# Attention, mixer and MLP kernel on one core: block sums written into V by ScalarE for every pair, and the second products moved one step later

## The chip, the core and the metric

The kernel runs on one NeuronCore of a Trainium2 chip. The metric is the device time of one execution in microseconds (us), the median of several runs. The engines have queues of their own and work through them in order: PE (TensorE, matrix products; its weight loads are a row of their own, PEld), ACT (ScalarE), DVE (VectorE), POOL (GpSimd) and SP (SyncE, which here issues nearly all DMAs). An instruction that waits holds up everything behind it on its engine.

## The reference

```python
def _attn_ref(q, k, v):                      # B, H, S, D = 2, 8, 768, 64
    block, window = (32, 16)
    k_sum = k.reshape(B, H, nb, block, D).max(axis=3)
    v_sum = v.reshape(B, H, nb, block, D).mean(axis=3)
    scores_l = scale * np.matmul(q, k.transpose(0, 1, 3, 2))      # kept where |i - j| < window
    scores_s = scale * np.einsum('bhsd,bhnd->bhsn', q, k_sum) + np.log(block)
    a = softmax over the local and the block scores together (+ 1e-09 below the line)
    return np.matmul(a, np.concatenate([v, v_sum], axis=2))

def _moe_ref(x, w_tok1, w_tok2, w_ch1, w_ch2):                   # d_tok, d_ch = 256, 1536
    h = np.maximum(x.transpose(0, 2, 1) @ w_tok1, 0.0) @ w_tok2
    u = x + h.transpose(0, 2, 1)
    return u + np.maximum(u @ w_ch1, 0.0) @ w_ch2

def _moe2_ref(x, g_ln, w_ch1, w_ch2):
    xn = layer norm of x, times g_ln
    return x + np.maximum(xn @ w_ch1, 0.0) @ w_ch2               # 512 -> 2048 -> 512
```

The output is `_moe2_ref(_moe_ref(attention))`. The weights arrive as 64-bit values.

## The kernel before

**Two stages.** First comes attention, woven with the token mixer of the first half; then a long run of products for the two MLPs. The 2 x 8 heads are worked off as 8 pairs (i = 0 to 7), two heads at a time, and each pair in three steps of 256 queries; so there are 24 steps (n = 0 to 23, pair i has n = 3i to 3i+2). What is called scores(n), exp(n) and so on below is the work of step n.

**One step.** PE multiplies Q by K and the block maxima of K into `scores` (16 matmuls, line 297). DVE adds the mask and takes the minimum (`sn`, `mn`, line 317), ACT takes the exponentials (`pr`, four instructions, line 327), PE transposes them (`pt`, line 334), ACT copies them to SBUF (`PT`, line 341, "evac"), PE multiplies them by V (`av`, 16 matmuls, line 354), DVE divides (`u`, line 371), and ACT and POOL split the result in a high and a low part (`xh`, `xl`, lines 385 and 394).

**V and the block sums.** V of a pair lies in one of three buffers, 121 rows x 2 sides x 6 windows. 96 rows of each side are loaded by DMA; the other 24 are the means of V over blocks, the same in all 6 windows. For them POOL adds up the transposed V (`VT`, line 252) into `Z`, PE transposes `Z` into PSUM (`psv`, line 261), and then: for pairs 0 and 1, ACT writes V directly with four instructions, one for each side and head (line 265); for pairs 2 to 7, ACT writes a small tile `VS` (line 274), and two DMAs on SP's queue repeat it over the 6 windows (line 281). Column 64 of those rows holds ones, for the sum of the weights.

**Weights.** They come in 62 halves of 512 KB (`stage`, line 165), through three buffers. Each half needs an ACT instruction (`dec`, line 113), four on DVE (lines 127, 129, 131, 135), one more on ACT (`wh`, line 175) and one more on DVE (`wl`, line 182). Half h+3 can be asked for only when line 135 of half h is done.

**The order** of PE, ACT, DVE and POOL in attention is written out by hand: every piece of a step has an offset in the table `ORDER`, the piece of step n stands at n + offset, and everything is sorted by that number. `evac` 1.4 and `av` 1.95 mean that the copy stands before exp of the next step (n + 1.5) and that av(n) stands before scores(n+2). SP's queue is not written out by hand. With each normalisation up to `ops` conversion pieces of the weights are woven in on DVE and ACT. From `bg` on, products of the token mixer (`g`, lines 198 to 200; the first pieces use the first three halves of weights) fill PE's free time; until then PE gets idle products with a constant tile (`fill`, `warm_ps`, line 616), two and three a step.

Of the kernel before, what the change touches and what calls it, by code (L numbers as in the profile page):

```python
# [10 lines left out]
F32 = mybir.dt.float32  # L11
F32R = mybir.dt.float32r
U32 = mybir.dt.uint32
AF = mybir.ActivationFunctionType
# [4 lines left out]
P = 128  # L19
B, H, S, D = 2, 8, 768, 64  # L20
BLOCK, WINDOW = 32, 16
NB = S // BLOCK
# [4 lines left out]
NK = 96 + NB  # L27
# [4 lines left out]
LEAD = 3  # L32
NXN = 3
ORDER = {
    "load_k": -5.2, "load_vt": -5.1, "load_v": -5.0, "kmax": -1.3, "copy_k": -1.0, "vsum": -2.4,
    "vput": -0.2, "vsum0": 0.6, "vput0": 1.12, "exp": 0.5, "tr": 1.1, "evac": 1.4, "av": 1.95,
    "norm": 2.6, "hi": 2.65, "lo": 2.7, "conv": 3.5, "bg": 9.3, "fin": 0.9,
}
GN = GT * P
NG = B * ST // GT  # L40
# [12 lines left out]
class Kern:  # L53
# [202 lines left out]

    def prep_v2(self, i):
        nc = self.nc
        V, Z, VS = self.V[i % 3], self.Z[i % 2], self.VS[i % 2]
        ps = self.ps_pt.tile([P, 512], F32, tag="pt", name=f"psv{i}")  # L260
        nc.tensor.transpose(ps[:NK, 0:P], Z, self.ident)
        if i < 2:
            for a, j in ((0, 0), (96, 1)):
                for r in range(2):
                    nc.scalar.activation(
                        V[a : a + NB, j, :, 65 * r : 65 * r + 64],
                        ps[a : a + NB, r * 64 : r * 64 + 64]
                        .rearrange("p (o n) -> p o n", o=1)
                        .to_broadcast([NB, 6, 64]),
                        AF.Copy,  # L270
                        scale=1.0 / BLOCK,
                    )
            return
        nc.scalar.activation(
            VS.rearrange("p (r c) -> p r c", r=2)[:, :, 0:64],
            ps[:NK, 0:P].rearrange("p (r c) -> p r c", r=2),
            AF.Copy,
            scale=1.0 / BLOCK,
        )
        for a, j in ((0, 0), (96, 1)):  # L280
            nc.sync.dma_start(
                V[a : a + NB, j, :, 0:129],
                VS[a : a + NB, 0:129].rearrange("p (o n) -> p o n", o=1).to_broadcast([NB, 6, 129]),
            )

    def att_qk(self, n):
# [274 lines left out]
    def attention(self):  # L561


        npair, nq = B * NPAIR, 3 * B * NPAIR
        O = ORDER
        ev = []
        put = lambda at, *fns: ev.append((at, len(ev), fns))
        for i in range(npair):
            at = 3 * i
            if i > 1:  # L570
                put(at + O["load_k"], lambda i=i: self.load_pair(i))
                put(at + O["load_vt"], lambda i=i: self.load_vt(i))
                put(at + O["load_v"], lambda i=i: self.load_v(i))
            put(at + (O["kmax"] if i != 1 else -0.45), lambda i=i: self.prep_k(i))
            put(at + (O["copy_k"] if i != 1 else -0.44), lambda i=i: self.copy_k(i))
            put(at + O["vsum"] if i else O["vsum0"], lambda i=i: self.prep_v1(i))
            put(at + O["vput"] if i else O["vput0"], lambda i=i: self.prep_v2(i))
        for n in range(nq):
            put(n, lambda n=n: self.att_qk(n))
            if n < O["bg"]:  # L580
                put(n + 0.02, lambda: self.fill(2))
                put(n + 0.15, lambda: self.fill(3))
            put(n + O["exp"], lambda n=n: self.att_exp(n))
            put(n + O["tr"], lambda n=n: self.att_tr(n))
            put(n + O["evac"], lambda n=n: self.att_evac(n))
            put(n + O["av"], lambda n=n: self.att_av(n))
            put(n + O["norm"], lambda n=n: self.weave(self.att_norm(n), self.convert(self.ops)))
            put(n + O["hi"], lambda n=n: self.att_hi(n))
            put(n + O["lo"], lambda n=n: self.att_lo(n))
        put(0.0, lambda: self.load_half(0), lambda: self.load_half(1))  # L590
        put(O["conv"], lambda: setattr(self, "ops", 3))
        put(O["bg"], lambda: setattr(self, "ops", 2))
        x0, x1, w0, w1 = self.g1(0, 0), self.g1(0, 1), self.g1(1, 0), self.g1(1, 1)
        y, z0 = self.g2(0), self.transpose_u(0)
        pieces = [x0, x0, x1, x1, y, y, y, y, w0, w0, z0, z0, z0, y, z0, w1, w1, y]
        low = {x0: 5 + O["lo"], x1: 11 + O["lo"], w0: 17 + O["lo"], w1: 23 + O["lo"]}
        need = {x0: 3, x1: 3, w0: 3, y: 6}
        at = O["bg"]
        for k, g in enumerate(pieces):
            while at < low.get(g, 0):  # L600
                at += 1
            if g in need:
                put(at, lambda g=g: self.convert_until(need[g]))
            put(at, lambda g=g: self.begin(g))
            put(at + O["fin"], lambda g=g: self.end(g))
            at += 1
        for _, _, fns in sorted(ev, key=lambda e: e[:2]):
            for fn in fns:
                fn()
        while self.evacs:  # L610
            self.end(self.evacs[0])
# [21 lines left out]
    def run(self):  # L633
        tc, nc, ctx = self.tc, self.nc, self.ctx
# [26 lines left out]
        att = self.att  # L661
# [1 line left out]
        self.K = [att.tile([P, 7, 184], F32, name=f"K{i}") for i in range(3)]  # L663
        self.PT = [att.tile([NK + 1, 512], F32, name=f"PT{i}") for i in range(2)]
        self.V = [att.tile([NK + 1, 2, 6, VC], F32, name=f"V{i}") for i in range(3)]
        self.VS = [att.tile([NK, 130], F32, name=f"VS{i}") for i in range(2)]
        self.VT = [att.tile([P, S], F32, name=f"VT{i}") for i in range(2)]
        self.Z = [att.tile([P, NK], F32, name=f"Z{i}") for i in range(2)]
        self.u = const.tile([P, B * ST, C], F32, name="u")
# [9 lines left out]
        nc.vector.memset(self.warm, 0.0)  # L679
        for t in self.Z:  # L680
            nc.gpsimd.memset(t, 0.0)
        for t in self.V[:2]:
            nc.gpsimd.memset(t[0:NB, 0, :, 64:65], 1.0)
            nc.gpsimd.memset(t[96:NK, 1, :, 64:65], 1.0)
        for t in self.VS:
            nc.gpsimd.memset(t[:, 64:65], 1.0)
        for t in self.PT:
            nc.vector.memset(t[96 : NK + 1], 1.0)
        self.load_pair(0, nc.scalar)
# [45 lines left out]
        for n in range(len(units) + 1):  # L735
# [3 lines left out]
            if n < len(units):  # L739
                kind, s, f, g = units[n]  # L740
                nf = F1 if kind == "u" else F2
                c = 3 + f if kind == "u" else 3 + F1 + f
# [117 lines left out]
```

## Time and profile before

| | |
|---|---|
| time, median of 3 runs | 607.97 us (607.54 to 608.3) |
| profiled execution | 609.79 us, its span 608.0 us |
| PE busy | 581.4 us, 96% of the span |
| DVE busy | 334.8 us, 55% |
| ACT busy | 202.3 us, 33% |
| POOL busy | 42.5 us, 7% |
| mean granted TensorE clock | 0.983 of full speed |

The span is what the profile sees of one execution, from the first instruction to the last; the time of that execution holds 1.8 us more around it. Attention ends about 107 us after the start, and nearly everything behind it is PE at full clock without a gap. So the shares of the whole page are those of the long last part, and attention has to be read by stretches.

### The profile page before, as it was taken

Reading aid. Unit: us, or ns where it says so; the run is one execution under the profiler, and the core shown is the slowest. Engines: PE = TensorE matmul, PEld = TensorE weight load, DVE = VectorE, ACT = ScalarE, POOL = GpSimd, SP = SyncE. Lnnn points to the kernel's source line nnn. Section 1 sums busy time; section 2 is a strip of 40 time slices with the busy share of each in tenths; the row PEclk is TensorE's granted clock in tenths of the full one; section 3 lists DMA queues with packets and bytes.
Section 4 is the critical chain, followed back from the end, with each engine's and each line's share of the span. In section 5 each row is a group of like instructions: output and inputs, shape, how many; then the busy total and the mean of one; then the engine's idle time right before and its main releaser. Section 6 shows DMA issues by size and latency. Waiting matters only on the chain.

```text
span 608.0 us, 9196 instructions
## 1 busy us (share of the span) xinstructions
PE 581.4 (96%) x3595; PEld 507.7 (84%) x3601; DVE 334.8 (55%) x847; ACT 202.3 (33%) x448; POOL 42.5 (7%) x78
## 2 busy tenths in 40 slices
PE   6849899999999999999999999999999999999997
PEld 2527677779899889999888989999888989999896
DVE  3576995899368799788789951111153211111122
ACT  4665877644133444343444411110122111010110
POOL 0443552000000000000000000000000000000000
PEclk9888899999999999999999999999999999999999
DMA  9996770135324333233423200000000100000011
GB/s 263 310 275 194 240 237 26 43 132 172 105 71 138 105 103 112 98 110 133 137 72 103 71 2 1 0 1 0 1 29 24 53 0 1 1 0 1 0 53 52
DMA packets 23377, 52.70 MB, mean 87 GB/s; under 512 B 2147, under 2 KB 10275, under 8 KB 23334
## 3 DMA queue, kind: packets, MB, share of 16 engines
q1 hardware_dynamic: 23184, 51.71, 27.2%
q8 instruction: 28, 0.46, 0.3%
q10 hardware_dynamic: 150, 0.41, 0.2%
q14 instruction: 15, 0.12, 0.1%
HBM read 48.08 MB, written 3.15 MB: 84 GB/s over the span
## 4 chain that ended last, share of the span: by engine, by line
PE 87%; DVE 6%; DMA 4%; ACT 1%; issue 1%; SPq 0%; ACTq 0%
DMA V<-VS 2%; PE g L198 1%; PE av L354 1%; PE g L200 1%; PE g L199 1%; DMA V<-in_v_dram 1%; DVE sn L317 1%; PE scores L297 1%; PE pt L334 1%; DMA mask<-in_mask_dram 1%; PE warm_ps L616 1%; PE tx L515 1%; DVE dec L135 1%; DVE dec L131 1%; PE acc_('x', 0)_0_3743 L199 1%
## 5 line engine op out<-in xcount | busy, mean ns | idle before, releaser
L113 ACT ACTIVATE dec<-stage 128x512 f32<-128x512 f32 x62 | 41.6, 673 | 11.0 <-DMA stage<-in_wts_dram 11.0
L135 DVE SCALAR_TENSOR_TENSOR dec<-stage,dec 128x512 uint32<-128x512 uint32 x62 | 44.0, 709 | 0.9
L131 DVE SCALAR_TENSOR_TENSOR dec<-stage,dec 128x512 uint32<-128x512 uint32 x62 | 43.8, 706 | 0.9
L175 ACT CAST wh<-dec 128x512 fp32r<-128x512 f32 x62 | 38.0, 615 | 17.1 <-DVE dec L135 16.9
L182 DVE TENSOR_TENSOR wl<-dec,wh 128x512 fp32r<-128x512 f32 x62 | 42.9, 695 | 0.0
L354 PEld LDWEIGHTS av<-V,PT 121*64 121x64 f32 x384 | 15.5, 152 | 23.6 <-issue 12.0
L354 PE MATMUL av<-V,PT 121*64 121x65 f32 x384 | 19.2, 243 | 16.2 <-DMA V<-VS 7.5
L317 DVE CUSTOM_DVE_ANT_0 sn<-scores,mask 128x120 f32<-128x120 f32 x96 | 21.2, 275 | 18.0 <-PE scores L297 18.0
L327 ACT ACTIVATE pr<-sn,mn 128x120 f32<-128x120 f32 x96 | 30.0, 386 | 2.7 <-DVE mn L317 2.6
L129 DVE TENSOR_SCALAR dec<-dec 128x512 uint32<-128x512 uint32 x62 | 28.0, 453 | 1.0
L127 DVE TENSOR_SCALAR dec<-dec 128x512 f32<-128x512 f32 x62 | 26.8, 433 | 1.8 <-ACT dec L113 1.8
L394 POOL TENSOR_TENSOR xl<-u,xh 128x256 fp32r<-128x256 f32 x24 | 18.9, 788 | 44.4 <-ACT xh L385 41.9
L616 PE MATMUL warm_ps<-warm 128*128 128x512 bf16 x59 | 19.2, 441 | 2.0 <-DVE warm L679 1.2
L252 POOL TENSOR_TENSOR VT<-VT 128x384 f32<-128x384 f32 (+3 forms) x28 | 19.0, 680 | 22.2 <-DMA VT<-in_vt_dram 20.6
L341 ACT COPY PT<-pt 120x512 f32<-120x512 f32 x24 | 14.0, 584 | 16.0 <-PE pt L334 15.8
L297 PE MATMUL scores<-K,Q 64*64 64x120 f32 x384 | 16.7, 293 | 1.9 <-ACT K L236 1.7
L334 PE MATMUL pt<-ident,pr 128*120 128x128 f32 x96 | 16.9, 300 | 0.0
L334 PEld LDWEIGHTS pt<-ident,pr 128*120 128x120 f32 x96 | 11.8, 148 | 5.1 <-issue 2.2
L198 PE MATMUL g<-xh,wh 128*128 128x256 f32 x48 | 14.2, 296 | 0.6 <-DVE u L431 0.6
L297 PEld LDWEIGHTS scores<-K,Q 64*64 64x64 f32 x384 | 10.8, 142 | 4.6 <-ACT K L236 2.2
L490 DVE TENSOR_SCALAR xn<-u,mv,rs 128x128 f32<-128x128 f32 x48 | 13.9, 340 | 0.0
L199 PE MATMUL g<-xl,wh 128*128 128x256 f32 x48 | 13.4, 279 | 0.0
(3004 smaller groups left out, 1669.7 us busy)
## 6 DMA issues: line engine op xcount, KB each, us to landing
stage<-in_wts_dram SPq DMA_DIRECT2D x62, 512.0 KB, 3.3
V<-in_v_dram SPq DMA_DIRECT2D x16, 306.0 KB, 8.4
K<-in_k_dram SPq DMA_DIRECT2D x8, 480.0 KB, 6.5
VT<-in_vt_dram SPq DMA_DIRECT2D x8, 384.0 KB, 9.1
out_dram<-u SPq DMA_DIRECT2D x12, 256.0 KB, 2.1
Q<-in_q_dram SPq DMA_DIRECT2D x7, 384.0 KB, 8.5
V<-VS SPq DMA_DIRECT2D x12, 72.6 KB
Q<-in_q_dram ACTq DMA_DIRECT2D x1, 384.0 KB, 3.3
```

What stands on the lines that cost most here:

```text
L113: nc.scalar.activation(m, self.raw[n][:, :, 1].bitcast(F32), AF.Abs)
L127: nc.vector.tensor_scalar(m, m, MAG_LO, MAG_HI, op0=ALU.max, op1=ALU.min)
L129: nc.vector.tensor_scalar(mi, mi, 3, 0x3FFFFFF8, op0=ALU.logical_shift_left, op1=ALU.bitwise_and)
L131: nc.vector.scalar_tensor_tensor(mi, t[:, :, 1], 0xC0000000, mi, op0=ALU.bitwise_and, op1=ALU.bitwise_or)
L135: nc.vector.scalar_tensor_tensor(mi, t[:, :, 0], 29, mi, op0=ALU.logical_shift_right, op1=ALU.bitwise_or)
L175: self.nc.scalar.copy(self.slots[c if c < 16 else c - 16][0][:, s], x)
L182: self.nc.vector.tensor_tensor(wl[:, s], x, f32(wh[:, s]), op=ALU.subtract)
L297: nc.tensor.matmul(ps[cols, j, e, :NK], Q[rows, 64 * w : 64 * w + 64], K.rearrange("p v c -> p (v c)")[rows, a : a + NK], start=True, stop ...
L317: nc.vector.tensor_tensor_reduce(sn[:, u], ps[:, u % 2, u // 2, :NK], self.mask[:, mv], scale=-SCALE, scalar=3e38, op0=ALU.add, op1=ALU.mi ...
L327: nc.scalar.activation(pr[:, u], sn[:, u], AF.Exp, bias=mn[:, u : u + 1], scale=-1.0)
L334: nc.tensor.transpose(ps[:NK, u * P : u * P + P], pr[:, u], self.ident)
L354: nc.tensor.matmul(ps[64 * j : 64 * j + 64, e, 65 * r : 65 * r + 65], pt[:, u * P + 64 * (r ^ j) : u * P + 64 * (r ^ j) + 64], V[:, j, 2 * ...
```

## The change

The block sums of every pair are now written by ACT straight into V, with one instruction a side that covers both heads and all 6 windows (24 x 768 values); `VS`, its two DMAs a pair and its memsets go, and the third V buffer gets its column of ones at the start. In the order, `av` moves from 1.95 to 2.15 and `evac` from 1.4 to 1.55: av(n) now stands behind scores(n+2) and the transposes of step n+1, and the copy of step n behind exp(n+1). The first product pieces of the mixer start at 8.58 instead of 9.3 and end 0.97 instead of 0.9 behind their start, the load of V stands at -4.7 instead of -5.0, each early step has four idle products instead of five, and four conversion pieces a step are woven in instead of three until `bg`, then two as before.

```diff
-    "load_k": -5.2, "load_vt": -5.1, "load_v": -5.0, "kmax": -1.3, "copy_k": -1.0, "vsum": -2.4,
-    "vput": -0.2, "vsum0": 0.6, "vput0": 1.12, "exp": 0.5, "tr": 1.1, "evac": 1.4, "av": 1.95,
-    "norm": 2.6, "hi": 2.65, "lo": 2.7, "conv": 3.5, "bg": 9.3, "fin": 0.9,
+    "load_k": -5.2, "load_vt": -5.1, "load_v": -4.7, "kmax": -1.3, "copy_k": -1.0, "vsum": -2.4,
+    "vput": -0.2, "vsum0": 0.6, "vput0": 1.12, "exp": 0.5, "tr": 1.1, "evac": 1.55, "av": 2.15,
+    "norm": 2.6, "hi": 2.65, "lo": 2.7, "conv": 3.5, "bg": 8.58, "fin": 0.97,
...
         nc.tensor.transpose(ps[:NK, 0:P], Z, self.ident)
-        if i < 2:
-            for a, j in ((0, 0), (96, 1)):
-                for r in range(2):
-                    nc.scalar.activation(
-                        V[a : a + NB, j, :, 65 * r : 65 * r + 64],
...
-        nc.scalar.activation(
-            VS.rearrange("p (r c) -> p r c", r=2)[:, :, 0:64],
...
         for a, j in ((0, 0), (96, 1)):
-            nc.sync.dma_start(
-                V[a : a + NB, j, :, 0:129],
-                VS[a : a + NB, 0:129].rearrange("p (o n) -> p o n", o=1).to_broadcast([NB, 6, 129]),
+            nc.scalar.activation(
+                V[a : a + NB, j, :, 0:130].rearrange("p w (r c) -> p w r c", r=2)[:, :, :, 0:64],
+                ps[a : a + NB, 0:P]
+                .rearrange("p (o r c) -> p o r c", o=1, r=2)
+                .to_broadcast([NB, 6, 2, 64]),
+                AF.Copy,
+                scale=1.0 / BLOCK,
             )
...
                 put(n + 0.02, lambda: self.fill(2))
-                put(n + 0.15, lambda: self.fill(3))
+                put(n + 0.25, lambda: self.fill(2))
...
-        put(O["conv"], lambda: setattr(self, "ops", 3))
+        put(O["conv"], lambda: setattr(self, "ops", 4))
...
-        for t in self.V[:2]:
+        for t in self.V:
             nc.gpsimd.memset(t[0:NB, 0, :, 64:65], 1.0)
             nc.gpsimd.memset(t[96:NK, 1, :, 64:65], 1.0)
-        for t in self.VS:
-            nc.gpsimd.memset(t[:, 64:65], 1.0)
```

**ACT around the block sums of pair 2 (steps 4 to 7).** Before, from the first split of weights to the exponentials of step 6 (`pr_505`) and those of step 7 (`pr_567`):

```order
L175 CAST wh_70<-dec_350 128x512
L113 ACTIVATE dec_413<-stage_352 128x512
L385 CAST xh_116<-u 128x2x128
L236 COPY K_100<-ks_417 128x7x24
L341 COPY PT_101<-pt_440 120x512
L327 ACTIVATE pr_451<-sn_449,mn_450 128x120 x4
L385 CAST xh_116<-u 128x2x128
L274 ACTIVATE VS_106<-psv_470 120x2x64
L341 COPY PT_102<-pt_494 120x512
L327 ACTIVATE pr_505<-sn_503,mn_504 128x120 x4
L175 CAST wh_70<-dec_355 128x512
L113 ACTIVATE dec_524<-stage_410 128x512
```

After, the same stretch, up to the exponentials of step 6 (`pr_497`) and the copy behind them:

```order
L175 CAST wh_70<-dec_340 128x512
L113 ACTIVATE dec_402<-stage_342 128x512
L371 CAST xh_114<-u 128x2x128
L236 COPY K_100<-ks_408 128x7x24
L313 ACTIVATE pr_440<-sn_438,mn_439 128x120 x4
L327 COPY PT_101<-pt_422 120x512
L175 CAST wh_70<-dec_345 128x512
L113 ACTIVATE dec_458<-stage_398 128x512
L371 CAST xh_114<-u 128x2x128
L263 ACTIVATE V_105<-psv_465 24x6x2x64 x2
L313 ACTIVATE pr_497<-sn_495,mn_496 128x120 x4
L327 COPY PT_102<-pt_479 120x512
```

Three things moved: each copy to `PT` stands behind the next step's exponentials, the two wide writes of V stand where the one of `VS` stood, and `dec` of the fourth half of weights (`stage_410` before, `stage_398` after; half 3 when counted from 0) now stands ahead of the exponentials of step 6 instead of behind them.

**PE in steps 10 to 12, around the block sums of pair 4 (`psv`).** There are no idle products here. Before, from the products with V of step 9 (`av_797`) on; the names after `pr` are those of steps 10 and 11:

```order
L354 MATMUL av_797<-V_103,PT_102 64x65 x8
L297 MATMUL scores<-K_98,Q_95 64x120 x8
L334 MATMUL pt_815<-ident,pr_773 120x128 x4
L261 MATMUL psv_841<-ident,Z_110 120x128
L354 MATMUL av_846<-V_103,PT_101 64x65 x8
L297 MATMUL scores<-K_99,Q_96 64x120 x8
L334 MATMUL pt_863<-ident,pr_825 120x128 x4
```

After, from the scores of step 11 on:

```order
L283 MATMUL scores<-K_98,Q_95 64x120 x8
L320 MATMUL pt_796<-ident,pr_760 120x128 x4
L340 MATMUL av_801<-V_103,PT_102 64x65 x8
L261 MATMUL psv_829<-ident,Z_108 120x128
L283 MATMUL scores<-K_99,Q_96 64x120 x8
L320 MATMUL pt_841<-ident,pr_812 120x128 x4
L340 MATMUL av_846<-V_103,PT_101 64x65 x8
```

The products with V of step 9 (`av_797`, now `av_801`) moved behind the scores of step 11 and the transposes of step 10, and those of step 10 behind the scores of step 12 and the transposes of step 11. Of the mixer's products, the first piece now stands between av(6) and `psv` of pair 3, ahead of scores(9), and the second ahead of scores(10); before they stood one step later, behind scores(9) and behind scores(10).

**SP's queue at pair 4.** Before:

```order
L165 DMA stage_410<-in_wts_dram 128x1024
L208 DMA K_99<-in_k_dram 128x6x160
L209 DMA Q_96<-in_q_dram 128x768
L165 DMA stage_466<-in_wts_dram 128x1024
L281 DMA V_105<-VS_106 24x6x129 x2
L213 DMA VT_108<-in_vt_dram 128x768
```

After:

```order
L165 DMA stage_398<-in_wts_dram 128x1024
L208 DMA K_99<-in_k_dram 128x6x160
L165 DMA stage_453<-in_wts_dram 128x1024
L209 DMA Q_96<-in_q_dram 128x768
L213 DMA VT_106<-in_vt_dram 128x768
L165 DMA stage_516<-in_wts_dram 128x1024
```

The two DMAs from `VS` are gone, and the loads of weights stand somewhat further ahead among those of K, Q and VT; the load of half 3 keeps its place behind the same DMAs.

## Rows read from the trace of the kernel before

**Rows 1.** Stretches: length, busy PE, PEld, DVE, ACT, POOL, PE clock, DMA share, GB/s.

```profile
30.00:37.00 7.00, 5.24 (x80) 3.70 (x82) 6.93 (x28) 5.54 (x16) 4.40 (x7) 1.00 1.06 290
37.00:45.20 8.20, 0.68 (x4) 0.12 (x2) 5.40 (x16) 3.71 (x10) 2.90 (x6) 0.77 1.06 272
45.20:51.00 5.80, 5.45 (x41) 3.59 (x42) 3.13 (x14) 1.91 (x7) 0.72 (x1) 0.50 0.53 142
51.00:62.00 11.00, 10.96 (x150) 9.27 (x150) 7.26 (x29) 8.23 (x24) 5.38 (x9) 0.97 0.78 229
62.00:81.00 19.00, 16.04 (x223) 13.60 (x223) 19.00 (x71) 14.69 (x40) 10.90 (x17) 0.91 0.80 236
81.00:100.00 19.00, 18.85 (x270) 15.32 (x268) 15.39 (x73) 13.82 (x41) 7.83 (x12) 1.00 0.50 149
100.00:110.00 10.00, 8.13 (x104) 5.99 (x97) 6.04 (x28) 7.04 (x20) 2.50 (x4) 1.00 0.01 2
```

**Rows 2.** Timeline of PE: start, duration, line, instruction, idle time before and its releaser.

```profile
30.41 0.32 PE L261 MATMUL psv<-ident,Z 128*120 128x128 f32 x1 [0.91 <-POOL Z L255]
...
45.21 1.59 PE L354 MATMUL av<-V,PT 121*64 121x65 f32 x16 [7.53 <-DMA V<-VS]
46.73 1.08 PE L297 MATMUL scores<-K,Q 64*64 64x120 f32 x16
...
51.94 0.64 PE L297 MATMUL scores<-K,Q 64*64 64x120 f32 x16
...
55.98 0.28 PE L200 MATMUL g<-xh,wl 128*128 128x256 f32 x1
```

**Rows 3.** Timeline of SP's DMA issues: start, duration, line, transfer.

```profile
26.64 0.33 SPq L220 DMA_DIRECT2D V<-in_v_dram  x1
29.27 0.35 SPq L165 DMA_DIRECT2D stage<-in_wts_dram  x1
...
34.36 2.60 SPq L281 DMA_DIRECT2D V<-VS  x2
```

**Rows 4.** Timeline of POOL in attention.

```profile
26.65 3.22 POOL L252 TENSOR_TENSOR VT<-VT 128x384 f32<-128x384 f32 x4 [4.62 <-DMA VT<-in_vt_dram]
29.95 0.41 POOL L255 TENSOR_TENSOR Z<-VT 128x24 f32<-128x24 f32 x2
```

**Rows 5.** Timeline of ACT around the block sums of pair 2.

```profile
34.64 1.25 ACT L327 ACTIVATE pr<-sn,mn 128x120 f32<-128x120 f32 x4
...
38.47 0.67 ACT L113 ACTIVATE dec<-stage 128x512 f32<-128x512 f32 x1 [2.06 <-DMA stage<-in_wts_dram]
39.04 0.39 ACT L385 CAST xh<-u 128x256 fp32r<-128x256 f32 x1
39.34 0.58 ACT L341 COPY PT<-pt 120x512 f32<-120x512 f32 x1
39.81 1.25 ACT L327 ACTIVATE pr<-sn,mn 128x120 f32<-128x120 f32 x4
40.97 0.60 ACT L175 CAST wh<-dec 128x512 fp32r<-128x512 f32 x1
44.59 0.66 ACT L113 ACTIVATE dec<-stage 128x512 f32<-128x512 f32 x1 [3.02 <-DMA stage<-in_wts_dram]
```

**Rows 6.** Groups of ACT by line and shape, 0 to 110 us: count, busy us, mean ns.

```profile
L265 ACT ACTIVATE V<-psv 24x384 f32<-24x384 f32 x8 | 3.4, 476 | 1.3 <-PE psv L261 1.2
...
L236 ACT COPY K<-ks 128x168 f32<-128x168 f32 x8 | 2.6, 329 | 1.1 <-DVE ks L226 1.0
...
L274 ACT ACTIVATE VS<-psv 120x128 f32<-120x128 f32 x6 | 1.7, 275 | 0.5 <-PE psv L261 0.4
```

**Rows 7.** What DVE waited for from 25.3 to 94 us: total, times, longest.

```profile
DVE sn L317 <- PE scores L297: 7.1, 3, 5.4
DVE hl L414 <- ACT hh L413: 2.0, 2, 1.3
```

**Rows 8.** What PE waited for from 25.3 to 110 us.

```profile
PE av L354 <- ACT PT L341: 5.6, 8, 1.8
```

More of the change, by code (lines that the diff above doesn't have):

```diff
@@ L258, in prep_v2 @@
         nc = self.nc
-        V, Z, VS = self.V[i % 3], self.Z[i % 2], self.VS[i % 2]
+        V, Z = self.V[i % 3], self.Z[i % 2]
         ps = self.ps_pt.tile([P, 512], F32, tag="pt", name=f"psv{i}")
         nc.tensor.transpose(ps[:NK, 0:P], Z, self.ident)
-        if i < 2:
-            for a, j in ((0, 0), (96, 1)):
-                for r in range(2):
-                    nc.scalar.activation(
-                        V[a : a + NB, j, :, 65 * r : 65 * r + 64],
[L267 to L273, printed above, removed]
-        nc.scalar.activation(
-            VS.rearrange("p (r c) -> p r c", r=2)[:, :, 0:64],
[L276 to L279, printed above, removed]
-        for a, j in ((0, 0), (96, 1)):
-            nc.sync.dma_start(
-                V[a : a + NB, j, :, 0:129],
-                VS[a : a + NB, 0:129].rearrange("p (o n) -> p o n", o=1).to_broadcast([NB, 6, 129]),
+        for a, j in ((0, 0), (96, 1)):
+            nc.scalar.activation(
[5 more added lines that the diff above has]
+                scale=1.0 / BLOCK,
             )
@@ L665, in run @@
         self.V = [att.tile([NK + 1, 2, 6, VC], F32, name=f"V{i}") for i in range(3)]
-        self.VS = [att.tile([NK, 130], F32, name=f"VS{i}") for i in range(2)]
         self.VT = [att.tile([P, S], F32, name=f"VT{i}") for i in range(2)]
```

## The prediction

> **What bounds the kernel now.** I read the table of stretches first [rows 1], because the page's shares are those of the long last part: there PE is busy without a gap, none of its instructions changes, and only the moment at which attention lets go of it counts. The reader is to see four kinds of stretch. From 30 to 37 us DVE is full (6.93 of 7.00 us). From 37 to 45.2 PE does almost nothing (0.68 us) while the DMA engines are full. From 62 to 81 DVE is full again (19.00 of 19.00). From 81 to 100 PE is (18.85 of 19.00).
>
> The timeline of PE names the hole [rows 2]: av(6), the first products that use pair 2's V, wait 7.53 us for the two DMAs from `VS`. These were issued from 34.36 on [rows 3] and had landed at 45.21. They move little, but stand in the queue behind bulk loads. After the hole PE's granted clock is 0.50, the lower level of 1.2 GHz, up to 51 us [rows 1]. The third view is who waits for whom on DVE [rows 7]: from 25.3 to 94 us it stood still for scores or for `hh` for 9.1 us in all (7.1 + 2.0), 5.4 of them in this hole. So 9.1 us is all that could be had there while DVE's work stays as it is.
>
> **What the change removes.** Twelve DMAs on SP, and with them the 7.53 us wait. The Trainium skill (DMA: Bandwidth & Descriptors, Anatomy of one DMA) fits one DMA, on the path from GpSimd, as about 2.0 us plus bytes / 436e3; for 72.6 KB that is an estimate of 2.2 us, the sums would be in V before PE asks for them, the first term below would be nothing, and the result some 606.5. The rows do not bear that out: 10.85 us passed between issue and release.
>
> **What it adds.** Two ACT instructions of 24 x 768 a pair. No row shows that shape. Of the nearest rows, both from PSUM, 128 values take 275 ns and 384 take 476 ns [rows 6], so one value more costs 0.785 ns, and 768 take 476 + 384 x 0.785 = 777 ns. Two are 1.5 us with a little overlap. From below it is two of the 384-value rows, 0.95 us; from above four of them, 1.9 us. I take 1.5. For pairs 2 to 7 that is 1.2 us more than `VS`, each time ahead of the exponentials; for pairs 0 and 1 some 0.3 us less.
>
> **What it moves, and where the stall goes.** Four conversion pieces a step instead of three put `dec` of weight half 3 ahead of exp(6), and behind it on ACT stand `xh`, the two V writes of pair 2, exp(6) and copy(5); PE's transposes of step 6 wait for that exp, and all that follows on PE for them. Half 3 was asked for at 29.27 [rows 3], and ACT got it at 38.47 after waiting 2.06 us [rows 5]. Before, that `dec` stood behind exp(6), which ran at 34.64. Asking a little earlier hardly helps: the same loads stand ahead of it, V of pair 3 issued up to 26.64 the last [rows 3]. I keep 38.47.
>
> From there, in starting distances of [rows 5]: `dec` 0.57, `xh` 0.30, V 1.5, exp 1.16, so exp(6) ends at 42.0, where before PE was let go at 45.21. Then copy 0.47, `wh` 0.5, `dec` of half 4 0.57, `xh` 0.30, exp 1.16: exp(7) ends at 45.0. Half 4 landed at 44.59; now it stands directly behind K of pair 4, and at the 272 to 290 GB/s of [rows 1] these 1.0 MB take 3.6 us, so it is there at 42.1. Half 5 stands behind Q and VT, 1.3 MB or 4.7 us more: 46.8, 0.8 us after ACT could take it. So `xh`(5) ends at 47.7, POOL's `xl` at 48.4 by the 0.7 us that I estimate for it, and the first product piece of the mixer, now ahead of scores(9), can run from there. Its 2.1 us are an estimate from 18 products of some 0.12 us, and `psv` and scores(9) take 0.9 more: scores(9) is done at 51.4. Before it was done at 52.5 (51.94 + 0.57), and the first product piece at 56.2 [rows 2]. With the transposes of step 8 and av(7), which before stood ahead of that (1.1 us), the new order is there at 52.5. The gain up to here is 3.7; I take 3.5, since PE comes out of a hole of its own at the lower clock too: behind `psv` at 30.7 it has scores(6), transposes, av(4) and scores(7) to do, some 4 us, and then waits from about 35 to 42. Bounds: nothing, and 9.1 us.
>
> Pairs 0 to 2 bring nothing before that: `psv` of pair 2 waits for POOL, POOL for the load of VT, which landed at 26.65, and `Z` was done at 30.36 [rows 2, 4]. None of it is moved.
>
> **From 62 to 81 us.** ACT is busy 14.69 us. Two pairs add 2.4, and the half of weights that is now handled earlier takes some 1.2 away (0.67 + 0.60, [rows 5]): 15.9. DVE loses five pieces of that half, some 3 us (an estimate at the 0.6 of ACT's instructions of that size): 16. PE has 16.04. So the 19 us cannot fall by more than 3. That ACT's copy no longer stands between the transposes and the next exponentials lets the three engines run side by side more, yet three engines that are 85% full get in each other's way: I take half, 1.5, with bounds 0 and 3.
>
> **From 81 to 100** PE is full: nothing. The V writes of pairs 6 and 7 lie beside PE's products there; ACT has 13.82 + 2.4 of 19. Without that cover they cost 2.4; I count 0.5 against. **From 100 to 110** PE is idle for 1.9 us (10.00 - 8.13), mostly for the copy to `PT` [rows 8], which is now off that path: 0.5, bounds 0 and 1.9.
>
> **Counted at nothing.** The 14 idle products that go: until 45 us PE waits anyway, and those of steps 8 and 9 are in the 3.7 above. The memsets: POOL waits for VT then [rows 4]. V's load at -4.7: it has to follow av, which is later by as much, and SP issues it behind the same kind of loads. K's copy (329 ns, [rows 6]) keeps its place ahead of an exp.
>
> **Sum.** 3.5 + 1.5 - 0.5 + 0.5 = 5.0 us. Against the profiled execution: 609.79 - 5.0 = 604.8, its span 603.0. That execution lay 1.8 us above the median of 607.97, so the forecast for the median is 603.0.
>
> **Rivals.**
> *All of it comes back.* Half 3 does not hold ACT up, or ACT has slack enough, and DVE runs full from 25 us on. Then up to 9.1 us return [rows 7] and 0.5 at the end: 607.97 - 9.6 = 598.4. For it speaks that DVE's total does not grow; against it the 2.06 and 3.02 us that ACT already waited for weights [rows 5]. The Trainium skill (DMA: Bandwidth & Descriptors, Queues, rings and completion order) says that each engine takes descriptors in ring order; by that rule half 3 cannot pass what was issued ahead of it, and the trace agrees with 9.2 us from issue to use. Chance 0.20.
> *Swallowed.* PE restarts sooner, but DVE, full from 62 to 81, and ACT with 2.4 us more give it back: -0.5 to +1.0, 607.5. For it speaks [rows 1], against it that DVE's idle time ahead of 62 is now used for weights. Chance 0.12.
> *ACT is the new bound, slower.* Place: `dec` of halves 3 to 5 ahead of exp(6) to exp(8), with V's writes in the same row. From 45.0 on each exp would wait for its half. It decides if half 3 comes after 42.0 (38.47 + 3.5); if half 5 then comes 6.1 us behind half 4, as 4 did behind 3 (44.59 - 38.47), it is there at 50.7 instead of 46.8, scores(9) is done 3.9 us later, and of the 3.7 us nothing is left (-0.2). From 62 to 81 ACT, now the bound, pays the 2.4 us of V writes in full: 607.97 + 0.2 + 2.4 = 610.6. Against it: the DMA engines lose the narrow `VS` transfers, in whose stretch the rate fell from 290 to 272 [rows 1]. Chance 0.11.
>
> **How the numbers follow.** The forecast has 0.57. A measurement of this kernel can tell 0.2% from no change (1.2 us, 606.8 to 609.2). Faster: 0.57 + 0.20 = 0.77; same 0.12; slower 0.11. The range is 598.5 to 607.0: it leaves out the slower case, about half of the swallowed one and the far end of the first rival, some 0.2 in all. The likeliest case alone lies within 600.5 to 605.5.
>
> **What would show it.** Right: no wait on `VS`; V writes of about 0.78 us; ACT waiting for `stage` ahead of exp(6), which ends near 42; a hole on PE from about 35 to 42; scores(9) near 51, with the first product piece ahead of it; the end of attention about 5 us sooner. Wrong: no such wait on ACT (then the first rival), ACT full from 62 to 81 with PE waiting for `pr` (then the second), or V writes well above 1 us.

## The result, and the profile after

The kernel after takes 615.57 us (median of four, 613.32 to 618.51), the kernel before, measured beside it, 608.13 us: ratio 1.0125 (95% interval 1.0101 to 1.0149). It is slower by 1.25%, some 7.6 us, where 5 us less was forecast.

The profiled execution after took 613.32 us, with a span of 611.5; it is the fastest of its four. The one of before [rows 1] took 609.79 us, and all four measured executions of before lie below that. So the two profiles are only 3.5 us apart, less than half of what lies between the medians. The same stretches as in [rows 1], columns as there:

```profile
30.00:37.00 7.00, 3.25 (x42) 1.60 (x40) 5.40 (x19) 2.36 (x5) 0.59 (x1) 0.91 1.05 301
37.00:45.20 8.20, 6.73 (x66) 4.36 (x67) 6.72 (x18) 7.10 (x18) 5.17 (x9) 0.66 0.76 254
45.20:51.00 5.80, 5.80 (x71) 5.18 (x70) 3.65 (x22) 5.63 (x14) 2.16 (x3) 1.00 0.97 350
51.00:62.00 11.00, 5.96 (x93) 4.34 (x92) 8.12 (x33) 7.55 (x22) 2.66 (x7) 0.74 0.75 221
62.00:81.00 19.00, 15.89 (x204) 12.47 (x202) 16.34 (x64) 14.06 (x36) 11.40 (x17) 0.88 0.67 215
81.00:100.00 19.00, 17.94 (x227) 13.55 (x228) 11.62 (x57) 14.57 (x37) 6.28 (x11) 1.00 0.13 35
100.00:110.00 10.00, 8.63 (x126) 6.51 (x126) 5.47 (x28) 7.46 (x21) 2.18 (x3) 1.00 0.01 2
```

The hole of PE from 37 to 45 is gone (6.73 us busy instead of 0.68). A new one stands from 51 to 62: PE is busy 5.96 of 11.00 us there, before 10.96. From 62 to 81 DVE is no longer full (16.34 of 19.00 us, before 19.00), yet PE does no more there than before (15.89, before 16.04).

Start by start the two profiled executions tell the same. Scores(10) begins at 51.06, before at 56.80: 5.7 us ahead. Scores(12) is 2.6 ahead (60.58 against 63.18), scores(15) 1.8 (73.02 against 74.86), scores(17) 1.1 behind (83.19 against 82.08), and the end of attention 3.15 behind (112.92 against 109.77; taken here and below as the start of the first product on `xh` behind the last `u`, line 198). So the lead lies ahead of step 10, 6.8 us of it go between steps 10 and 17, and 2 more from there to the end. The lead is one over a slow execution: in two more of the kernel before, shown further down, scores(10) begins at 50.94 and 54.42. The place of the loss is seen on ACT (start, duration, line, instruction, idle time before):

```profile
48.59 1.63 ACT L263 ACTIVATE V<-psv 24x768 f32<-24x768 f32 x2
50.24 1.25 ACT L313 ACTIVATE pr<-sn,mn 128x120 f32<-128x120 f32 x4
51.52 0.59 ACT L327 COPY PT<-pt 120x512 f32<-120x512 f32 x1
52.00 0.39 ACT L399 ACTIVATE hh<-g 128x256 fp32r<-128x256 f32 x1
53.62 0.40 ACT L371 CAST xh<-u 128x256 fp32r<-128x256 f32 x1 [1.23 <-DVE u L357]
54.42 1.25 ACT L313 ACTIVATE pr<-sn,mn 128x120 f32<-128x120 f32 x4 [0.40 <-DVE mn L303]
55.57 0.56 ACT L327 COPY PT<-pt 120x512 f32<-120x512 f32 x1
56.04 0.38 ACT L399 ACTIVATE hh<-g 128x256 fp32r<-128x256 f32 x1
...
59.94 1.25 ACT L313 ACTIVATE pr<-sn,mn 128x120 f32<-128x120 f32 x4
```

and on DVE in the same time:

```profile
52.42 0.42 DVE L400 SCALAR_TENSOR_TENSOR hl<-g,hh 128x256 fp32r<-128x256 f32 x1 [3.57 <-ACT hh L399]
52.76 0.17 DVE L354 RECIPROCAL rec<-av 128x4 f32<-128x4 f32 x1
52.85 0.40 DVE L129 TENSOR_SCALAR dec<-dec 128x512 uint32<-128x512 uint32 x1
53.16 0.42 DVE L357 TENSOR_TENSOR u<-av,rec 128x256 f32<-128x256 f32 x1
53.50 0.68 DVE L131 SCALAR_TENSOR_TENSOR dec<-stage,dec 128x512 uint32<-128x512 uint32 x1
54.10 0.28 DVE L303 CUSTOM_DVE_ANT_0 sn<-scores,mask 128x120 f32<-128x120 f32 x1
...
56.45 0.42 DVE L400 SCALAR_TENSOR_TENSOR hl<-g,hh 128x256 fp32r<-128x256 f32 x1 [1.46 <-ACT hh L399]
```

`hh` and `hl` take the high and low part of a mixer piece. With `bg` 8.58 and `fin` 0.97 they stand at 9.55: on ACT behind the exponentials (9.5) and behind the copy of the step, on DVE still ahead of `sn` of the next step. So the two engines take turns. DVE waits for `hh`; then come `hl`, the division and two weight pieces, and only then `sn`; ACT meanwhile waits for `sn`. One turn, from exp to exp, takes 4.18 us (50.24 to 54.42), and the next 5.52 (54.42 to 59.94). The kernel before was no quicker in its first turn here:

```profile
54.07 1.26 ACT L327 ACTIVATE pr<-sn,mn 128x120 f32<-128x120 f32 x4
...
58.55 1.25 ACT L327 ACTIVATE pr<-sn,mn 128x120 f32<-128x120 f32 x4
...
62.55 1.25 ACT L327 ACTIVATE pr<-sn,mn 128x120 f32<-128x120 f32 x4
```

Its two turns took 4.48 and 4.00 us, but PE was full with product pieces of the mixer then (10.96 of 11.00 us). In the kernel after the first of these pieces lies behind already, and PE waits with the others:

```profile
51.06 0.64 PE L283 MATMUL scores<-K,Q 64*64 64x120 f32 x16
...
55.05 0.64 PE L283 MATMUL scores<-K,Q 64*64 64x120 f32 x16 [2.14 <-DVE mn L303]
...
60.58 1.08 PE L283 MATMUL scores<-K,Q 64*64 64x120 f32 x16 [2.85 <-ACT pr L313]
...
82.06 0.51 PE L198 MATMUL g<-hh,wh 128*128 128x512 f32 x1 [1.24 <-ACT hh L399]
```

The last row is the second product of the mixer, which needs `hh` at once and holds up scores(17) behind it on PE's queue.

### The profile page after: what moved, and what is told of

Its sections match the earlier page's. It is cut to its first block, busy times and chain, and to the rows that moved or that the text cites. A ratio compares the mean times of both kernels' runs of the same rounds, so it can differ in the third digit from the quotient of the medians.

```text
span 611.5 us, 9137 instructions
## 1 busy us (share of the span) xinstructions
PE 583.8 (95%) x3587; PEld 505.2 (83%) x3587; DVE 334.0 (55%) x847; ACT 210.5 (34%) x450; POOL 41.3 (7%) x78
## 3 DMA queue, kind: packets, MB, share of 16 engines
HBM read 48.08 MB, written 3.15 MB: 84 GB/s over the span
## 4 chain that ended last, share of the span: by engine, by line
PE 84%; ACT 5%; DMA 4%; DVE 4%; issue 1%; POOL 0%; SPq 0%; ACTq 0%; POOLq 0%
ACT pr L313 2%; DMA stage<-in_wts_dram 2%; PE g L198 1%; DMA VT<-in_vt_dram 1%; PE g L199 1%; PE g L200 1%; PE tx L501 1%; PE av L340 1%; DMA mask<-in_mask_dram 1%; ACT PT L327 1%; PE scores L283 1%; PE pt L320 1%; ACT V L263 1%; PE acc_('x', 0)_0_3717 L199 1%; PE acc_('x', 2)_0_4718 L199 1%
## 5 line engine op out<-in xcount | busy, mean ns | idle before, releaser
L283 PEld LDWEIGHTS scores<-K,Q 64*64 64x64 f32 x384 | 10.8, 142 | 17.4 <-DVE mn L303 5.4
L320 PE MATMUL pt<-ident,pr 128*120 128x128 f32 x96 | 18.5, 312 | 5.8 <-ACT pr L313 4.7
L320 PEld LDWEIGHTS pt<-ident,pr 128*120 128x120 f32 x96 | 11.8, 149 | 12.6 <-ACT pr L313 6.9
L602 PE MATMUL warm_ps<-warm 128*128 128x512 bf16 x51 | 17.1, 451 | 1.2 <-DVE warm L664 1.2
L263 ACT ACTIVATE V<-psv 24x768 f32<-24x768 f32 x16 | 12.9, 808 | 4.0 <-PE psv L261 4.0
```

What stands on the lines that cost most here:

```text
L283: nc.tensor.matmul(ps[cols, j, e, :NK], Q[rows, 64 * w : 64 * w + 64], K.rearrange("p v c -> p (v c)")[rows, a : a + NK], start=True, stop ...
L320: nc.tensor.transpose(ps[:NK, u * P : u * P + P], pr[:, u], self.ident)
```

## The experiments

Each version was measured beside the kernel before; ratios are to that, with a 95% interval. The diffs show the numbers or lines that change; the rest of a longer line is left out. Four theories stood at the start. **M**: the mixer's places, `hh` above all, are the loss. **A**: the V writes on ScalarE are. **O**: the fourth conversion piece is. **S**: weight loads on SP's queue behind waiting VT and V loads are.

### Which part of the change costs

**V writes alone.** After, with everything else back (the diff gathers numbers that stand on several lines):

```diff
-"load_v": -4.7, "evac": 1.55, "av": 2.15, "bg": 8.58, "fin": 0.97   # fill 2+2, ops 4
+"load_v": -5.0, "evac": 1.4, "av": 1.95, "bg": 9.3, "fin": 0.9      # fill 2+3, ops 3
```

> Only the V writes by ScalarE are changed; every place in the order, the fills and the conversion pieces a step are those of before. Theory M (the loss lies in the mixer's places: hh now stands behind V writes, exp and copy, and VectorE's hl waits for it): the 7.5 us wait goes and nothing is given back, 601 to 604 us. Theory A (the V writes on ScalarE ahead of every third exp are the loss, 1.6 us a pair): 609 to 614 us, and ScalarE is what PE waits for from 62 to 81 us.

Measured 607.1 us, 0.9992 (0.9969 to 1.0014): both missed. The V writes and the removed wait together change nothing that can be measured.

**New places alone**, V sums over `VS` as before (the diff above the other way round, in the kernel before):

> All places in the order, the fills and the four conversion pieces are those of after; the V sums still go over VS and twelve DMAs. Theory M: the new places cost some 6 us on top of the old wait for VS, 611 to 616 us. Theory A: without the V writes on ScalarE the new places do no harm, 604 to 608.5 us.

Measured 614.05 us, 1.0113 (1.0088 to 1.0138): as M said. The new order (places, fills and pieces) carries nearly all of the loss without any V write, so A falls.

**After with the mixer's old places.**

```diff
-"bg": 8.58, "fin": 0.97,
+"bg": 9.3, "fin": 0.9,
```

> After with the two numbers of the mixer's pieces as before (9.3 and 0.9 in place of 8.58 and 0.97). Theory M: hh stands ahead of the exp of its step again, hl waits about 1.5 us less twice, and the time falls to 603 to 609 us. Theory S (weight loads stand on SP behind VT and V loads that wait for GpSimd and PE) or theory O (a fourth conversion piece a step fills ScalarE and VectorE too early): 612 to 616 us, as after.

Measured 611.12 us, 1.0059 (1.0040 to 1.0077): between the two, about half of the loss.

**After with three conversion pieces.**

```diff
-put(O["conv"], lambda: setattr(self, "ops", 4))
+put(O["conv"], lambda: setattr(self, "ops", 3))
```

> After with three conversion pieces a step up to the mixer, as before. Theory O: the 4.6 us wait of dec ahead of exp(6) and the crowding behind it go, 605 to 610 us. Theory M or S: less weight work is done early, and the time stays at 613 to 617 us.

Measured 611.92 us, 1.0080 (1.0055 to 1.0106): between again. So neither M in this form nor O explains all of it, and the question is whether the parts add up.

### One number

**After with `hh` ahead of the exponentials.** The pieces' products stay where they are.

```diff
-"bg": 8.58, "fin": 0.97,
+"bg": 8.58, "fin": 0.9,
```

> After with one number changed: a mixer piece's hh and hl at 0.90 instead of 0.97 behind its products, which puts hh ahead of the exp and the copy of that step. Theory M: most of what the old mixer's places gave back (4.5 us) comes with this number alone, 609.5 to 612.5 us. Rival: what counts is where the products of a piece stand on PE, and not hh, 614 to 617 us.

Measured 608.62 us, 1.0007 (0.9989 to 1.0026): the whole loss is gone, more than M expected. ACT in this kernel:

```profile
51.96 0.39 ACT L399 ACTIVATE hh<-g 128x256 fp32r<-128x256 f32 x1
53.04 1.25 ACT L313 ACTIVATE pr<-sn,mn 128x120 f32<-128x120 f32 x4 [0.69 <-DVE mn L303]
54.20 0.56 ACT L327 COPY PT<-pt 120x512 f32<-120x512 f32 x1
54.66 0.40 ACT L371 CAST xh<-u 128x256 fp32r<-128x256 f32 x1
54.97 0.38 ACT L399 ACTIVATE hh<-g 128x256 fp32r<-128x256 f32 x1
56.03 1.25 ACT L313 ACTIVATE pr<-sn,mn 128x120 f32<-128x120 f32 x4 [0.69 <-DVE mn L303]
...
59.68 1.25 ACT L313 ACTIVATE pr<-sn,mn 128x120 f32<-128x120 f32 x4
```

and DVE:

```profile
55.38 0.42 DVE L400 SCALAR_TENSOR_TENSOR hl<-g,hh 128x256 fp32r<-128x256 f32 x1 [0.43 <-ACT hh L399]
55.72 0.27 DVE L303 CUSTOM_DVE_ANT_0 sn<-scores,mask 128x120 f32<-128x120 f32 x1
```

The first turn from exp to exp takes 2.99 us instead of 4.18, the second 3.65 instead of 5.52: 6.64 us for both instead of 9.70. `sn` follows `hl` on DVE at once, and the division and the weight pieces run while ACT is at the exponentials. The number `fin` moves `hh` on ACT and `hl` on DVE together; the two were not moved apart. At the second product PE does not wait for `hh` at all.

**The same without V writes**: the new places with `VS` kept, and `fin` 0.9.

> All new places but hh at 0.90, with VS and its DMAs kept and no V write by ScalarE from pair 2 on. Theory M (the place of hh by itself): the 6.6 us of the new places (614.05) come back, 606 to 609.5 us. Rival (hh is late because V writes stand ahead of it; without them its place costs little, and the loss of 614.05 has another cause): 612 to 615 us.

Measured 608.21 us, 1.0003 (0.9983 to 1.0023), as M said. With `VS` and `hh` at 0.97 ACT shows

```profile
53.73 1.24 ACT L327 ACTIVATE pr<-sn,mn 128x120 f32<-128x120 f32 x4
54.87 0.56 ACT L341 COPY PT<-pt 120x512 f32<-120x512 f32 x1
55.33 0.38 ACT L413 ACTIVATE hh<-g 128x256 fp32r<-128x256 f32 x1
...
57.74 1.25 ACT L327 ACTIVATE pr<-sn,mn 128x120 f32<-128x120 f32 x4 [0.40 <-DVE mn L317]
```

and with `hh` at 0.90

```profile
53.69 1.25 ACT L327 ACTIVATE pr<-sn,mn 128x120 f32<-128x120 f32 x4 [0.69 <-DVE mn L317]
...
56.68 1.25 ACT L327 ACTIVATE pr<-sn,mn 128x120 f32<-128x120 f32 x4 [0.69 <-DVE mn L317]
```

a first turn of 4.01 us against 2.99. So the V writes have no part in the loss.

**`hh` early for the first two pieces only.**

```diff
-put(at + O["fin"], lambda g=g: self.end(g))
+put(at + (0.9 if k < 2 else O["fin"]), lambda g=g: self.end(g))
```

> After with hh at 0.90 for the first two mixer pieces alone, and at 0.97 for the other sixteen. If the loss lies at the first two (the trace of after loses its lead from step 11 on, behind their hh): 608 to 611 us. If it lies at the later ones: 613 to 616 us.

Measured 612.2 us, 1.0071 (1.0044 to 1.0099): between. The first two pieces carry 0.54 of the 1.18%, or 3.3 us, which fits the 3.1 us of the two turns; the later ones carry 0.64. Either share is uncertain by some 0.3. The later part shows on PE in this kernel, between scores(16) and scores(17):

```profile
80.32 0.50 PE L198 MATMUL g<-hh,wh 128*128 128x512 f32 x1 [2.61 <-ACT hh L399]
```

### Do the other parts add up?

**After with the old depth.**

```diff
-"load_v": -4.7, "evac": 1.55, "av": 2.15,
+"load_v": -5.0, "evac": 1.4, "av": 1.95,
```

> After with the copy, av and the V load at their old places (1.4, 1.95, -5.0). Theory D: 608 to 612 us. Theory M+O: the mixer's places and the fourth piece are still there, and PE's wait for PT comes back, 615 to 619 us.

Measured 623.04 us, 1.0232 (1.0200 to 1.0263), above what either expected. Theory D (the depth costs) falls; without it PE waits 15.8 us for `PT`, in after 1.4:

```profile
PE av L340 <- ACT PT L327: 15.8, 12, 4.8
```

**V writes and depth, mixer, fills and pieces as before.**

> V writes by ScalarE and the deeper places (copy 1.55, av 2.15, V load -4.7); mixer, fills and conversion pieces as before. Theory M+O (mixer's places and the fourth piece are the whole loss): PE no longer waits 10.8 us for PT as with the V writes alone, and 601 to 606 us come out. Theory D (the depth itself costs, because av, and with it V's release and the next V load, come later): 609 to 613 us.

Measured 608.25 us, 1.0002 (0.9983 to 1.0021): neither. The depth, worth 1.1% in the kernel after, is worth nothing with the mixer, fills and pieces as before (0.9992 without it). It takes PE's wait for `PT` away, and what it costs in exchange is seen late in attention: from scores(17) to the end of attention the kernel before takes 27.7 us in each of three profiles and the V writes alone 28.0, but four orders with the new depth take 29.0 to 29.8 us, the kernel with `hh` at 0.90 among them (29.8). Some 0.6 us of it is one more product with V, which stands behind scores(17) there. Why the rest comes was not looked into.

This version differs from "after with the mixer's old places" (1.0059) only in the three pieces and the fifth idle product a step. So where the mixer is late, four pieces with fewer idle products cost 0.6%; the two were not told apart.

**After with a third VT buffer** (`VT[i % 3]` and three tiles).

> After with a third VT buffer, so that no VT load waits on SP for GpSimd and the weight loads behind it are issued earlier. Theory S: dec waits less (9.1 us in all in after), scores(15) comes about 2 us earlier, 608 to 612 us. Theory M+O: 613.5 to 617 us.

Measured 612.17 us, 1.0068 (1.0045 to 1.0090): it gives back 0.6%, just above S's range. But with `hh` at 0.90 and three pieces, without and with the third buffer:

> After with hh at 0.90 and three conversion pieces. If the two losses are separate (each alone gave some 3.5 to 7 us back): 604 to 606.5 us. If both come from the same crowding on ScalarE around the first mixer piece: 607.5 to 609.5 us, no better than with 0.90 alone.

> The same with a third VT buffer, which gave 3 us in after. If separate from the other two: 600 to 604 us. If not: 606 to 609 us.

609.02 us, 1.0029 (1.0001 to 1.0056), and 608.51 us, 1.0012 (0.9989 to 1.0036). Against 1.0007 neither gives anything: with `hh` early there is nothing left for them to give back. So O and S are not needed for the loss of the change as it was made. That the fourth piece does no harm anywhere is not shown: with the mixer's old places it costs 0.6%, as said above.

### Why the removed wait brings nothing

**The kernel before, again**, twice:

> The kernel before, unchanged, against itself: what a comparison of two equal kernels gives, and a second profile. Theory T (the profiled execution of before, 609.79 us, was a slow one, and its wait for VS longer than usual): a ratio of 0.998 to 1.002, and a wait for VS of 4 to 6 us. Rival: the wait is 7 to 8 us again, and what its removal gives is lost elsewhere.

> A third profile of the kernel before. Theory T: the wait for VS differs from execution to execution; 2 to 6 us here, and attention ends between 104 and 108 us. Rival (7.5 us is the rule and the second profile the exception): 7 to 8 us, and an end near 109.8 us.

Against itself it gave 0.9999 (0.9973 to 1.0024). The profiled executions took 604.6 us (span 602.8 and the 1.8 around it) and 607.76 us. PE's row of [rows 2] for av(6) in the second and in the third execution:

```profile
40.74 1.46 PE L354 MATMUL av<-V,PT 121*64 121x65 f32 x16 [3.20 <-DMA V<-VS]
```

```profile
44.17 1.40 PE L354 MATMUL av<-V,PT 121*64 121x65 f32 x16 [5.82 <-DMA V<-in_v_dram]
```

So the wait was 7.53, 3.20 and 5.82 us, av(6) began at 45.21, 40.74 and 44.17, and attention ended at 109.77, 104.46 and 107.62. The execution that I had read was the slowest of the three. The wait differs from execution to execution, as T said, though 3.20 us is less than T's 4 to 6. In the third the trace names the load of V as the last to arrive; the `VS` DMAs were issued at 32.97 there, 11.2 us ahead of av(6).

**V writes made small**: one window of six; the other sums are left out, and ones stand in their place.

```diff
-V[a : a + NB, j, :, 0:130] ... .to_broadcast([NB, 6, 2, 64])
+V[a : a + NB, j, 0:1, 0:130] ... .to_broadcast([NB, 1, 2, 64])
```

> The V writes alone, with each instruction writing the sums of one window instead of six (24x128 values; the sums of the other windows are left at 1, so the result is not the right one). Theory P (the time of the V writes on ScalarE, ahead of the copy to PT, eats what the removed wait gave): by 808 - 275 = 533 ns less for each of two instructions a pair, 1.07 us a pair, the time falls to 602 to 605 us. Rival (the removed wait was worth little to begin with): 606 to 608 us.

Measured 609.4 us, 1.0018 (0.9996 to 1.0040): no gain. The time of the V writes is not what eats it.

**V writes later.**

```diff
-"vput": -0.2,
+"vput": 0.6,
```

> The V writes alone, placed behind the exp of their step (0.6) instead of ahead of it and of the copy to PT (-0.2). Theory P: the copy and the exp no longer wait for 1.6 us, 603 to 606 us. Rival (ScalarE is full there, and whatever stands behind loses the same): 606.5 to 609 us.

Measured 612.92 us, 1.0085 (1.0053 to 1.0118): worse than both expected, so the new place has a cost of its own: PE waits 17.1 us for `PT`, with the V writes alone 10.8. P finds support in neither form.

**Three weight loads left out**, halves 0 to 2 converted a second time in their place.

```diff
+if 3 <= h < 6:
+    self.raw[h] = self.keep[h - 3]
```

> The V writes alone, and the loads of weight halves 3 to 5 left out: halves 0 to 2 stay in their buffers and are converted a second time, so that all instructions on the engines stay and 1.57 MB of loads go (the weights of these halves are not the right ones). Theory L (what the wait for VS held up is held up by the weight loads now: dec waits 7.8 us with the V writes alone): 600 to 603.5 us. Rival (VectorE and ScalarE have no room for more anyway): 606 to 608 us.

Measured 604.69 us, 0.9940 (0.9916 to 0.9964): 0.5% less than the V writes alone. That lies between the two ranges, 1.2 us above L's and 1.3 below the rival's: the loads are part of it, not all. With the V writes alone ACT stands still for weights, and the copy, exp and `hh` behind:

```profile
40.63 0.66 ACT L113 ACTIVATE dec<-stage 128x512 f32<-128x512 f32 x1 [1.71 <-DMA stage<-in_wts_dram]
...
45.87 0.68 ACT L113 ACTIVATE dec<-stage 128x512 f32<-128x512 f32 x1 [1.87 <-DMA stage<-in_wts_dram]
...
50.32 0.38 ACT L399 ACTIVATE hh<-g 128x256 fp32r<-128x256 f32 x1
```

Without these loads the same instructions run at 39.10 and 43.95, with no wait:

```profile
39.10 0.69 ACT L113 ACTIVATE dec<-stage 128x512 f32<-128x512 f32 x1
...
43.95 0.68 ACT L113 ACTIVATE dec<-stage 128x512 f32<-128x512 f32 x1
```

**The same loads later**, with nothing left out:

```diff
+seq = [0, 1, 2, None, None] + list(range(3, NHALF))   # order of the halves, turn by turn
```

> The V writes alone, and weight halves 3 and later asked for and converted two turns later (two empty turns behind half 2), with nothing left out. Theory L: the loads that dec waited for between 35 and 46 us come when the DMA engines have room, 603.5 to 605.5 us. Rival (the same work then crowds the steps from 62 us on, or the second product waits for its six halves): 607 to 612 us.

Measured 608.89 us, 1.0010 (0.9984 to 1.0036): no gain, as the rival said. The trace fits its reason: the last product of the mixer's second piece begins 2.6 us sooner than with the V writes alone (50.05 against 52.67), but 56.4 us pass from there to the end of attention instead of 52.9.

The same distance shows where the rest of the gain goes. The kernel before needs 50.0, 50.5 and 50.2 us for it in its three profiles (59.81 to 109.77 in the first). The V writes alone need 52.9, with small writes 52.8, without the three loads 53.3. So what the V writes win ahead of step 10 is given back behind it, 2.4 to 2.9 us, and neither the time of the writes nor these loads explain that part. Each is one execution, and the cause stays open.

No version beat the kernel before by more than can be measured, save the one that leaves loads out.

## Why the prediction was wrong, point by point

**The wait for `VS` goes: right.** No wait for `VS` is left. But its size was taken from one execution. Three executions of the same kernel show 7.53, 3.20 and 5.82 us; the first term (3.5 us) and the bound of 9.1 us [rows 7] were sized on the largest. The V writes alone changed the time by -0.5 us (-1.9 to +0.9), though with the old depth and three pieces, so that is not exactly this term. With every new place and `hh` early nothing is left of it either: 1.0007.

**The V writes: right.** I estimated 777 ns each; the group shows 808 ns, and a pair of them 1.63 us against 1.5:

```profile
L263 ACT ACTIVATE V<-psv 24x768 f32<-24x768 f32 x16 | 12.9, 808 | 4.0 <-PE psv L261 4.0
```

That they lie beside other work was right as well: made small in the version with the V writes alone, they bring nothing (1.0018).

**`dec` of half 3 ahead of exp(6): right in mechanism.** ACT waits for it, and PE's transposes wait behind. Both come earlier than I had it (38.47 and 42.0). "Asking a little earlier hardly helps" was wrong: half 3 was asked for at 25.47 instead of 29.27, and was there at 35.38 instead of 38.47:

```profile
35.38 0.66 ACT L113 ACTIVATE dec<-stage 128x512 f32<-128x512 f32 x1 [4.64 <-DMA stage<-in_wts_dram]
...
37.88 1.25 ACT L313 ACTIVATE pr<-sn,mn 128x120 f32<-128x120 f32 x4
```

```profile
38.33 1.33 PE L320 MATMUL pt<-ident,pr 128*120 128x128 f32 x4 [4.13 <-ACT pr L313]
```

So scores(9) was done at 47.6, not at 51.4, with the first product piece ahead of it as forecast. Up to step 10 the kernel was even better than I said, against that one execution. In the first rival I took the 9.2 us from issue to use as agreement on the order of descriptors; they show how long ACT had to wait, not in which order the transfers landed.

**From 62 to 81 us a gain of 1.5: wrong; this step failed.** I argued that the copy, no longer between the transposes and the next exponentials, "lets the three engines run side by side more". I had looked at where `exp`, the copy and the products go, and not at `hh` and `hl`, which `bg` and `fin` move too: I put no price on them, neither there nor under what is counted at nothing. 8.58 + 0.97 = 9.55 stands behind exp at 9.5, where 9.3 + 0.9 = 10.2 stood ahead of exp at 10.5. With that ACT and DVE take turns, which costs 3.1 us over the first two pieces (9.70 against 6.64), and PE waits at the second product. The runs put the whole at 6.7 us without and 7.2 us with the V writes (1.0113 - 1.0003 and 1.0125 - 1.0007, times 608). The loss begins at 51 us, ahead of the stretch in which I looked for it.

These 7.2 us are not all of the miss, which is 12.6 us (615.57 against 603.0). The other 5.4 are nearly all the forecast gain of 5.0 itself: with `hh` early the kernel is level with the one before, no faster. The first term was sized on the slowest of three executions, and what is won ahead of step 10 is given back behind it.

**From 81 to 100, PE is full, half a microsecond against: wrong.** PE is busy 17.94 of 19.00 us and waits for `hh` at 82.06. But `hh` is not all of it: from scores(17) on the new depth takes as long with `hh` early (29.8 us) as with it late (29.7), and 2 us longer than the kernel before. **The end, 0.5 for the copy: wrong.** PE's wait for `PT`, 5.6 us in [rows 8], fell to 1.4, yet from scores(23) to the end of attention the kernel after takes 9.14 us (103.78 to 112.92), the kernel before 7.69 (102.08 to 109.77). One more product with V, 0.6 us, stands there; the rest was not looked into.

**The rivals.** "ACT is the new bound, slower" had the right sign and the right engine, at 610.6, and the wrong place: neither `dec` nor the V writes, but `hh`. "Swallowed" (607.5) is what the kernel does once `hh` is early, 1.0007. Its cause is settled only in part: with the V writes alone, leaving three weight loads out gives 0.5% back, so the loads hold up some of what no longer waits for `VS`. Whether it is their traffic or only the moment at which they land was not told apart, and the kernel before was not run without them. It was not run with `hh` late either.

## What to carry to other kernels

In an order written by numbers, go through every event whose number passes another's, on each engine, and not only through those that the change is about: 9.55 against 9.5 cost 7.2 us, where the forecast gain was 5. An instruction that waits early on one engine for one that stands late on another can make the two take turns; look for a pair of waits that answer each other (DVE `hl` for ACT `hh`, ACT exp for DVE `sn`) and measure the turn. Take the size of a DMA wait from several executions before it goes into a sum. Follow a lead to the end of the stage before calling it a gain.

## What the runs showed of the hardware that was not expected

Three executions of the same kernel waited 3.20 to 7.53 us in the same place. From the issue of the first `VS` DMA to av(6) it took 10.85, 8.79 (31.95 to 40.74) and 11.20 us (32.97 to 44.17); in the last the trace names V's load as what came last, so there 11.20 only bounds the `VS` DMAs from above. The end of attention moved about as av(6) did: 5.3 us against 4.5 between the first execution and the second, 2.2 against 1.0 between the first and the third. The Trainium skill (ScalarE: Activation LUTs, What ACT_TABLE_LOAD costs) gives 186 ns plus 0.833 ns a column for such an ACT instruction, an estimate of 826 ns for 768; the trace agrees within 3% with 808, though each of these instructions repeats 128 values six times.
